# Transposing q, k and x in whole 128x128 blocks instead of 64x64 quarters, in a fused attention and mixture kernel

## The chip, the cores and the metric

The kernel runs on one core of a Trainium2 chip. The metric is the device time of one execution in microseconds (us), lower is better. A core has five engines that work side by side, each through a queue of its own in order: TensorE (PE, matrix products), ScalarE (ACT), VectorE (DVE), GpSimd (POOL) and SyncE (SP, which here only issues transfers). Matrix products read SBUF and write PSUM, a small memory of eight banks; ACT and DVE carry results from PSUM back to SBUF.

## The reference, cut to what matters

Three stages follow one another: an attention with decay over 4 batches, 8 heads, 768 tokens and 64 channels, a soft mixture of 8 experts, and a feed-forward layer with a gate. The change touches the first.

```python
for b in range(nb):                       # 12 blocks of 64 tokens
    intra = einsum('bhic,bhjc->bhij', qb, kb) * Dmask
    intra = einsum('bhij,bhjd->bhid', intra, vb)
    inter = einsum('bhid,bhde->bhie', qb * lam_pow, kv_state)
    out[:, :, sl] = intra + inter
    kv_state = lam_block * kv_state + einsum('bhsd,bhse->bhde', kb * rev_pow, vb)
x = out.transpose(0, 2, 1, 3).reshape(B * S, H * D)      # 3072 x 512
logits = x @ phi                                          # 32 slots, 4 for each of 8 experts
slot_input = softmax(logits, 0).T @ x                     # experts: relu(. @ w1[e]) @ w2[e]
x = softmax(logits, 1) @ slot_out
h = x @ w_in
out = (h * sigmoid(1.702 * h)) @ w_out
```

The scores need q and k with the channels on the partitions, though they lie in memory with the tokens there, so both are transposed on TensorE. The attention's result comes out with channels on the partitions and is transposed back.

## The kernel before

The attention is a loop of 48 steps. A step is 256 tokens of one batch and two heads: two chunks (c) of 128 tokens, each as two subs of 64 partitions by even and odd token. The loop is a pipeline written out by hand: iteration i works on steps i-1, i, i+1 and i+2 at once, and the order of the calls in it is the order of each engine's queue. On TensorE an iteration is, in this order:

- do_SC(i+1), L262: scores of step i+1 from qkT, the transposed q and k. do_ST(i+1), L278: what the step adds to the state, from kd (k times the decay) and v. Both write the banks bs.
- do_T(i+2), L235: q and k of step i+2 are transposed by products with an identity, 16 of them, each on one 64x64 quarter of the array, into the banks bt.
- do_XS(i), L301: q times the state, into the banks bx.
- do_XT(i-1), L327: the result x of step i-1 is transposed back, 8 products on quarters, into other columns of the same bt.
- in six of every eight iterations a piece of the mixture's head: L345 (logits), L355, L379, L394, L423 and L408.
- do_XA(i), L316: scores times v, into bx.

Around it ACT copies bt to qkT (take_T, L240) and to xn (take_XT, L335) and bx to xT (L321); DVE masks the scores (AT, L269) and adds the states (L285 to L291); POOL makes qdT (do_qd, L247) and kd (do_kd, L253), and a part of an early conversion of late weights in every fourth iteration (L195, L196). SP issues all loads: q, k and v of later steps, pieces of the expert weights w (NPC of them within the loop), and stage for the conversion. make_dec (L478, L481) fills the decay masks in the first iterations.

TensorE's float32 products are each two pairs of a weight load and a matmul in the trace (768 records at L316 for 8 products in 48 steps), a transpose through PE.transpose is one pair (20 records at L355 for 4 in 5 calls).

After the loop come the experts (L723, L745) and the feed-forward layer (L919, L966). The change leaves them as they are, but for one weight piece that is loaded a little later.

Of the kernel before, what the change touches and what calls it, by code (L numbers as in the profile page):

```python
# [8 lines left out]
F32 = mybir.dt.float32  # L9
F32R = mybir.dt.float32r  # L10
U32 = mybir.dt.uint32
AF = mybir.ActivationFunctionType
# [5 lines left out]
def attention_moe_gelu_kernel(  # L18
# [14 lines left out]
    PE, ACT, DVE, POOL, SP = nc.tensor, nc.scalar, nc.vector, nc.gpsimd, nc.sync  # L33

    B, H, S, D = q.shape
    P = 128
    NHP = H // 2
    HS = 384
    BT = 256
# [13 lines left out]
    NG = NBLK // UB  # L53
    NSTEP = NBLK * NHP
    NE = 1
    NPC = 31
    NPC_B = 6
    NPC_C = 4
    EPS = 1e-9
    TG = 2 * HS  # L60
# [22 lines left out]
    early = early_cm.__enter__()  # L83

    def bank(tag, name):
        return psp.tile([P, 512], F32, tag=tag, name=name)

    def banks(tag, name):
        return psp.tile([P, 2, 512], F32, tag=tag, name=name)

    ident = const.tile([P, P], F32, name="ident")
# [3 lines left out]

    dec = early.tile([P, H, 2, P], F32, name="dec", bufs=1)
    qtab = early.tile([P, NHP, 2, D], F32, name="qtab", bufs=1)
    for tag, n, bufs in (("kd", BT, 2), ("qkT", 2 * BT, 2), ("k", BT, 4), ("q", BT, 4)):
        early.tile([P, n], F32, tag=tag, name="room", bufs=bufs)
    c_nat = const.tile([P, NT // P, NS], F32, name="c_nat")  # L100
    acc = const.tile([P, DM], F32, name="acc")
# [8 lines left out]
    q_t, k_t, v_t = {}, {}, {}  # L110
# [6 lines left out]
    def load_step(s, what="qkv"):  # L117
        if s >= NSTEP:
            return
        b, bb, hp, blk = step_of(s)  # L120
        for src, nm, ts, bufs, pool in ((q, "q", q_t, 4, early), (k, "k", k_t, 4, early), (v, "v", v_t, 5, attn)):
            if nm in what:
                t = ts[s] = pool.tile([P, 2, 2 * D], F32, tag=nm, name=nm, bufs=bufs)
                SP.dma_start(out=t, in_=src[b, 2 * hp:2 * hp + 2, bb * BT:(bb + 1) * BT, :]
                             .rearrange("h (p s) d -> p h (s d)", s=2))
# [99 lines left out]


    s_mid, s_end = {}, {}
    qkT, qdT, kd, AT, xT, xn = {}, {}, {}, {}, {}, {}

    def do_T(s, bt):  # L230
        for j, src in enumerate((q_t[s], k_t[s])):
            for sub in range(2):
                for c in range(2):
                    for h in range(2):
                        PE.matmul(bt[HR[h], c, (2 * j + sub) * D:(2 * j + sub + 1) * D],  # L235
                                  src[HR[c], h, sub * D:(sub + 1) * D], ident[HR[c], HR[c]], start=True, stop=True)

    def take_T(s, bt):
        t = qkT[s] = early.tile([P, 2, 2, 2, D], F32, tag="qkT", name="qkT", bufs=2)
        ACT.activation(out=t.rearrange("m c j s p -> m c (j s p)"), in_=bt[:, :, :4 * D], func=AF.Copy)  # L240

    def do_qd(s):
        if s < 0 or s >= NSTEP:
# [6 lines left out]
    def do_kd(s):  # L250
        b, bb, hp, blk = step_of(s)
        kd[s] = early.tile([P, 2, 2, D], F32, tag="kd", name="kd", bufs=2)
        POOL.tensor_tensor(out=kd[s], in0=k_t[s].rearrange("q h (s d) -> q h s d", s=2),  # L253
                           in1=dec[:, 2 * hp:2 * hp + 2, :, P - 1:P].to_broadcast([P, 2, 2, D]), op=ALU.mult)

    HR = [slice(h * D, (h + 1) * D) for h in range(2)]
# [24 lines left out]
    def do_state(s, bs):  # L281
        b, bb, hp, blk = step_of(s)
        s_mid[s] = attn.tile([P, D], F32, tag="sm", name="sm")
        if bb == 0:
            DVE.tensor_copy(out=s_mid[s], in_=bs[:, 0, 2 * P:2 * P + D])  # L285
        else:
            DVE.scalar_tensor_tensor(out=s_mid[s], in0=s_end[s - NHP], scalar=qtab[:, hp, 1, D - 1:D],
                                     in1=bs[:, 0, 2 * P:2 * P + D], op0=ALU.mult, op1=ALU.add)
        if bb < NB - 1:
            s_end[s] = attn.tile([P, D], F32, tag=f"se{hp}", name="se")  # L290
            DVE.scalar_tensor_tensor(out=s_end[s], in0=s_mid[s], scalar=qtab[:, hp, 1, D - 1:D],  # L291
                                     in1=bs[:, 1, 2 * P:2 * P + D], op0=ALU.mult, op1=ALU.add)
# [27 lines left out]
        xT[s] = tailp.tile([P, 2, P], F32, tag="xT", name="xT", bufs=NHP + 1)  # L320
        ACT.activation(out=xT[s], in_=bx[:, :, :P], func=AF.Copy)  # L321

    def do_XT(s, bt):
        for c in range(2):
            for u in range(2):
                for h in range(2):
                    PE.matmul(bt[HR[u], h, (4 + c) * D:(5 + c) * D], xT[s][HR[h], c, HR[u]], ident[HR[h], HR[h]],  # L327
                              start=True, stop=True)

    def take_XT(s, bt):  # L330
        b, bb, hp, blk = step_of(s)
        g, half = divmod(blk, UB)
        if hp == 0 and half == 0:
            xn[g] = tailp.tile([P, R, NHP, P], F32, tag="xn", name="xn")
        ACT.activation(out=xn[g][:, 2 * half:2 * half + 2, hp].rearrange("p c (h d) -> p h c d", h=2),  # L335
                       in_=bt[:, :, 4 * D:6 * D].rearrange("p h (c d) -> p h c d", c=2), func=AF.Copy)


    RS = R * NS
# [111 lines left out]
    with tc.manual_schedule():  # L451
# [36 lines left out]
        n = 1  # L488
# [3 lines left out]
            n *= 2  # L492
        load_step(1, "v")
        load_step(2, "qk")
        POOL.memset(ones, 1.0)

        def make_isum():
# [10 lines left out]
        for i in range(-2, NSTEP):  # L508
            g, ph = divmod(i, PH)
            if i == 1:  # L510
                make_isum()
            if 0 < i + 2 < NHP:
                for h in range(2):
                    make_dec(2 * (i + 2) + h)

            load_step(i + 5, "qk")
            load_step(i + 4, "v")
            load_pieces(i)
            if i == -2:
                SP.dma_start(out=phi_sb, in_=phi.rearrange("(k p) s -> p k s", p=P))  # L520
            c, turn = divmod(i - 2, EVERY)
            if turn == 1 and 0 <= c + 1 < len(EARLY):
                load_early(c + 1)

            bs, bt, bx = banks("s", "bs"), banks("t", "bt"), banks("x", "bx")
            if 0 <= i + 1 < NSTEP:
                do_SC(i + 1, bs)
                do_ST(i + 1, bs)
                take_SC(i + 1, bs)
                do_state(i + 1, bs)  # L530
            if 0 <= i + 2 < NSTEP:
                do_T(i + 2, bt)
                if i == -2:
                    warm_up(1)
            if 0 <= i < NSTEP:
                fence = do_XS(i, bx)
            if 0 <= i - 1 < NSTEP:
                do_XT(i - 1, bt)
            if 0 <= i + 2 < NSTEP:
                take_T(i + 2, bt)  # L540
            if 0 <= i - 1 < NSTEP:
                take_XT(i - 1, bt)
            do_qd(i + 1)
            if 0 <= i + 2 < NSTEP:
                do_kd(i + 2)
            if ph == 0 and 0 <= g - 1 < NG:
                tail_logits(g - 1, 1)
            if ph == 4 and 0 <= g < NG:
                tail_logits(g, 0)
            if ph == 1 and 0 <= g - 1 < NG:  # L550
                tail_L(g - 1)
            if ph == 2 and 0 <= g - 1 < NG:
                tail_max(g - 1)
            if ph == 3 and 0 <= g - 1 < NG:
                tail_exp(g - 1)
            if ph == 5 and 0 <= g - 1 < NG:
                tail_z(g - 1)
                tail_slot(g - 1)
            if i == NSTEP - 1:
                tail_logits(NG - 1, 1, NHP - 1)  # L560

            if 0 <= i < NSTEP:
                do_XA(i, bx, fence)
            if ph == 5 and 0 <= g - 1 < NG:
                tail_acc(g - 1)

            if turn == 0 and 0 <= c < len(EARLY):
                do_early(c)
            if ph == 4 and 0 <= g - 1 < NG:
                tail_row(g - 1)  # L570
            if ph == 6 and 0 <= g - 1 < NG:
                tail_row_exp(g - 1)
            if i == NSTEP - 2:
                early_cm.__exit__(None, None, None)
                slotb_cm = tc.tile_pool(name="slotb", bufs=NPC_B, side="right", reuse_waits="tile")
                slotb = slotb_cm.__enter__()

                rooms = [piece_room(NPC + j) for j in reversed(range(NPC_B))]
                while rooms:
                    load_piece(rooms.pop())  # L580
            if i == NSTEP - 1:
                attn_cm.__exit__(None, None, None)
                slotc_cm = tc.tile_pool(name="slotc", bufs=NPC_C, side="left", reuse_waits="tile")
                slotc = slotc_cm.__enter__()
                for _ in range(NPC_C):
                    load_piece()
# [48 lines left out]
        DVE.tensor_reduce(out=cm, in_=bL[:, :RS].rearrange("p (c s) -> p s c", c=R), axis=AX.X, op=ALU.max)  # L635
        L = tl["L", g] = tailp.tile([P, R, NS], F32, tag="lp", name="L", bufs=1)
        DVE.tensor_copy(out=L, in_=bL[:, :RS].rearrange("p (c s) -> p c s", c=R))
        bt = banks("t", "bt")
        do_XT(NSTEP - 1, bt)
        take_XT(NSTEP - 1, bt)  # L640
        psa_cm.__exit__(None, None, None)
        psp = ctx.enter_context(tc.tile_pool(name="psp", bufs=1, space=bass.MemoryType.PSUM, reuse_waits="tile"))

# [443 lines left out]
```

## Time and profile before

| what | us |
|---|---|
| median of three runs (543.84 to 546.93) | 545.87 |
| the profiled execution's own time | 546.3 |
| its span, first to last instruction | 544.5 |
| TensorE busy (92% of the span) | 498.2 |
| VectorE, ScalarE, GpSimd busy | 251.7, 240.6, 91.8 |
| mean granted TensorE clock, as a share of full | 0.971 |

A busy TensorE is one on which some matmul is shown to run; the ends of matmuls are modelled, and a stall begins within such an end. "Issue" in a row is time in which an engine waited for nothing that the profile shows.

### The profile page before, as it was taken

What the parts mean: (1) busy time and instruction counts of PE and PEld (TensorE: products, weight loads), DVE (VectorE), ACT (ScalarE), POOL (GpSimd) and SP (SyncE); (2) the same over time, 40 slices, a digit from 0 to 9 for tenths busy, and PEclk for the clock granted to TensorE, in tenths of its full rate; (3) what the DMA queues carried; (4) which work ended last, traced back from release to release, by engine and by line L of the source; (5) the groups of instructions that cost most, each with busy time, mean ns of one, the idle gap of its engine ahead of it and who ended that gap; (6) DMA issues with size and microseconds to landing.
All of it is one profiled execution on the core that took longest, in us unless ns stands there. A gap on an engine that the chain in (4) does not pass through costs nothing.

```text
span 544.5 us, 15920 instructions
## 1 busy us (share of the span) xinstructions
PE 498.2 (92%) x6846; PEld 392.3 (72%) x6846; DVE 251.7 (46%) x503; ACT 240.6 (44%) x495; POOL 91.8 (17%) x166
## 2 busy tenths in 40 slices
PE   5778787988877789999999999999999999999997
PEld 3667676776756564447878778888888888888886
DVE  5543344454535332128979999732225222522222
ACT  3433333434323332348768777543333333333333
POOL 3544544545435311000000000000000000000000
PEclk7899999989989988999999999999999999999999
DMA  6587766778757598983444353030003000300003
GB/s 172 147 250 203 232 203 200 211 224 250 203 173 201 175 334 321 395 333 108 125 154 153 119 155 116 0 117 0 1 0 117 1 2 0 117 0 1 0 1 116
DMA packets 62150, 76.60 MB, mean 141 GB/s; under 512 B 4992, under 2 KB 42112, under 8 KB 62080
## 3 DMA queue, kind: packets, MB, share of 16 engines
q1 hardware_dynamic: 61936, 75.58, 43.6%
q8 instruction: 54, 0.88, 0.7%
q14 instruction: 16, 0.13, 0.1%
q10 hardware_dynamic: 144, 0.00, 0.0%
HBM read 69.28 MB, written 6.29 MB: 139 GB/s over the span
## 4 chain that ended last, share of the span: by engine, by line
PE 78%; issue 10%; POOL 5%; DVE 4%; ACT 1%; DMA 1%; POOLq 0%; ACTq 0%; DVEq 0%
PE bo L966 47%; PE bhh L919 4%; PE bh L723 3%; PE bx L316 3%; PE bt L235 3%; PE bs L262 3%; PE bacc L745 3%; PE bx L301 2%; PE bs L278 2%; PE bt L327 2%; POOL qdT L247 2%; POOL kd L253 1%; PE bl L345 1%; DVE seeds L478 1%; POOL isum L500 1%
## 5 line engine op out<-in xcount | busy, mean ns | idle before, releaser
L966 PE MATMUL bo<-whi,ghi 128*128 128x512 f32 x382 | 150.1, 395 | 0.1
L966 PE MATMUL bo<-whi,glo 128*128 128x512 f32 x382 | 149.7, 394 | 0.0
L966 PE MATMUL bo<-wlo,ghi 128*128 128x512 f32 x382 | 148.9, 391 | 0.1
L933 DVE TENSOR_TENSOR glo<-g,ghi 128x768 fp32r<-128x768 f32 x64 | 61.2, 956 | 132.4 <-ACT ghi L930 132.3
L927 ACT ACTIVATE g<-bhh 128x384 f32<-128x384 f32 x128 | 56.2, 489 | 125.9 <-PE bhh L919 125.8
L966 PEld LDWEIGHTS bo<-whi,glo 128*128 128x128 f32 x382 | 71.7, 188 | 16.7 <-DVE glo L933 0.3
L966 PEld LDWEIGHTS bo<-wlo,ghi 128*128 128x128 f32 x382 | 71.7, 188 | 16.3 <-issue 2.5
L966 PEld LDWEIGHTS bo<-whi,ghi 128*128 128x128 f32 x382 | 71.7, 188 | 13.9 <-DVE W2s L877 0.5
L240 ACT ACTIVATE qkT<-bt 128x512 f32<-128x512 f32 x48 | 28.8, 599 | 100.9 <-PE bt L327 99.3
L269 DVE TENSOR_TENSOR AT<-bs,dec 128x512 f32<-128x512 f32 x48 | 32.9, 686 | 67.2 <-PE bs L278 67.2
L930 ACT ACTIVATE ghi<-g 128x768 fp32r<-128x768 f32 (+1 forms) x65 | 54.4, 836 | 2.1
L247 POOL TENSOR_TENSOR qdT<-qkT,qtab 128x256 f32<-128x256 f32 x48 | 35.0, 730 | 51.2 <-ACT qkT L240 47.3
L262 PE MATMUL bs<-qkT 64*64 64x128 f32 x768 | 33.0, 286 | 10.5 <-ACT qkT L240 8.9
L327 PE MATMUL bt<-ident,xT 64*64 64x64 f32 x768 | 31.9, 234 | 7.7 <-issue 7.7
L316 PE MATMUL bx<-AT,v 64*64 64x128 f32 x768 | 35.5, 291 | 1.0 <-issue 0.6
L262 PEld LDWEIGHTS bs<-qkT 64*64 64x64 f32 x768 | 23.1, 138 | 16.0 <-ACT qkT L240 12.9
L919 PE MATMUL bhh<-cT,W2s 128*128 128x384 f32 x128 | 33.3, 338 | 0.0
L316 PEld LDWEIGHTS bx<-AT,v 64*64 64x64 f32 x768 | 23.4, 139 | 13.5 <-issue 11.9
L235 PE MATMUL bt<-ident,k 64*64 64x64 f32 x768 | 24.3, 229 | 8.5 <-issue 8.5
L253 POOL TENSOR_TENSOR kd<-k,dec 128x256 f32<-128x256 f32 x48 | 29.8, 621 | 9.1 <-ACT dec L481 6.5
L278 PE MATMUL bs<-v,kd 64*64 64x64 f32 x640 | 23.2, 231 | 8.2 <-issue 4.7
L327 PEld LDWEIGHTS bt<-ident,xT 64*64 64x64 f32 x768 | 24.8, 136 | 7.3 <-issue 7.3
(167 smaller groups left out, 633.3 us busy)
## 6 DMA issues: line engine op xcount, KB each, us to landing
w<-in_moe_w_dram SPq DMA_DIRECT2D x64, 512.0 KB, 5.2
f<-in_moe_w_out_dram SPq DMA_DIRECT2D x15, 512.0 KB, 3.6
q<-in_q_dram SPq DMA_DIRECT2D x48, 128.0 KB, 4.0
k<-in_k_dram SPq DMA_DIRECT2D x48, 128.0 KB, 3.7
v<-in_v_dram SPq DMA_DIRECT2D x48, 128.0 KB, 3.4
f<-in_moe_w_in_dram SPq DMA_DIRECT2D x12, 512.0 KB, 3.8
out_dram<-o SPq DMA_DIRECT2D x23, 256.0 KB, 2.1
stage<-in_moe_w_in_dram SPq DMA_DIRECT2D x8, 256.0 KB, 4.3
```

Source lines behind the costliest of these rows:

```text
L235: PE.matmul(bt[HR[h], c, (2 * j + sub) * D:(2 * j + sub + 1) * D], src[HR[c], h, sub * D:(sub + 1) * D], ident[HR[c], HR[c]], start=True, ...
L247: POOL.tensor_tensor(out=qdT[s], in0=qkT[s][:, :, 0], in1=qtab[:, hp, None].to_broadcast([P, 2, 2, D]), op=ALU.mult)
L253: POOL.tensor_tensor(out=kd[s], in0=k_t[s].rearrange("q h (s d) -> q h s d", s=2), in1=dec[:, 2 * hp:2 * hp + 2, :, P - 1:P].to_broadcast( ...
L262: PE.matmul(bs[HR[c], h, sj * P:(sj + 1) * P], qkT[s][HR[h], c, 1, sj], qkT[s][HR[h], c, 0].rearrange("m s p -> m (s p)"), start=True, sto ...
L278: PE.matmul(bs[HR[h], c, 2 * P:2 * P + D], kd[s][HR[c], h, sj, :], v_t[s][HR[c], h, sj * D:(sj + 1) * D], start=(sj == 0), stop=(sj == 1), ...
L316: mm = PE.matmul(bx[HR[h], c, :P], v_t[s][HR[c], h, sj * D:(sj + 1) * D], AT[s][HR[c], h, sj, :], start=(sj == 0 and c + bb == 0), stop=(s ...
L327: PE.matmul(bt[HR[u], h, (4 + c) * D:(5 + c) * D], xT[s][HR[h], c, HR[u]], ident[HR[h], HR[h]], start=True, stop=True)
L919: PE.matmul(bh[j][u][:, :HS], W2s[:, f * P:(f + 1) * P], cT[tg // (NTG // 2)][:, t0:t0 + HS], start=True, stop=True)
L927: ACT.activation(out=g[j][:, u * HS:(u + 1) * HS], in_=bh[j][u][:, :HS], func=AF.Gelu_apprx_sigmoid)
L930: ACT.activation(out=ghi[j][:, o], in_=g[j][:, o], func=AF.Copy)
L933: DVE.tensor_tensor(out=glo[j][:, o], in0=g[j][:, o], in1=ghi[j][:, o].bitcast(F32), op=ALU.subtract)
L966: PE.matmul(ob[t], a[j][:, t * P:(t + 1) * P], w[f], start=(begin and i == 0), stop=(end and i == 2))
```

## The change

q and k of a step are copied (do_qk), q by ACT and k by DVE, into a tile qk in which the 64 channels of both heads of a token stand side by side. A transpose of 128 tokens by 128 of these columns then gives both heads at once, so do_T is four whole 128x128 transposes and do_XT two. Each has a bank of its own (t and xt), where both shared the two banks bt. On TensorE do_T moves behind do_XS; on ACT take_T stands right behind do_T, take_XT moves behind the copy of xT, and the copy of q follows it; POOL's do_kd reads qk. q and k are loaded one step earlier, and one weight piece moves from the loop to its end.

```diff
-    NPC = 31
-    NPC_B = 6
+    NPC = 30
+    NPC_B = 7
...
-    def do_T(s, bt):
-        for j, src in enumerate((q_t[s], k_t[s])):
+    def do_qk(s):
+        if s >= NSTEP:
+            return
+        t = qk[s] = early.tile([P, 2, 2, 2, D], F32, tag="qk", name="qk", bufs=2)
+        ACT.activation(out=t[:, 0].rearrange("q s h d -> q h s d"),
+                       in_=q_t[s].rearrange("q h (s d) -> q h s d", s=2), func=AF.Copy)
+        DVE.tensor_copy(out=t[:, 1].rearrange("q s h d -> q h s d"),
+                        in_=k_t[s].rearrange("q h (s d) -> q h s d", s=2))
+
+    def do_T(s):
+        bt = bank("t", "bt")
+        for j in range(2):
             for sub in range(2):
-                for c in range(2):
-                    for h in range(2):
-                        PE.matmul(bt[HR[h], c, (2 * j + sub) * D:(2 * j + sub + 1) * D],
-                                  src[HR[c], h, sub * D:(sub + 1) * D], ident[HR[c], HR[c]], start=True, stop=True)
-
-    def take_T(s, bt):
+                PE.transpose(bt[:, (2 * j + sub) * P:(2 * j + sub + 1) * P],
+                             qk[s][:, j, sub].rearrange("q h d -> q (h d)"), ident)
         t = qkT[s] = early.tile([P, 2, 2, 2, D], F32, tag="qkT", name="qkT", bufs=2)
-        ACT.activation(out=t.rearrange("m c j s p -> m c (j s p)"), in_=bt[:, :, :4 * D], func=AF.Copy)
+        ACT.activation(out=t.rearrange("m c j s p -> m c (j s) p"),
+                       in_=bt.rearrange("m (j c p) -> m c j p", j=4, c=2), func=AF.Copy)
...
-        POOL.tensor_tensor(out=kd[s], in0=k_t[s].rearrange("q h (s d) -> q h s d", s=2),
+        POOL.tensor_tensor(out=kd[s], in0=qk[s][:, 1].rearrange("q s h d -> q h s d"),
...
-    def do_XT(s, bt):
+    def do_XT(s):
+        bt = bank("xt", "bxt")
         for c in range(2):
-            for u in range(2):
-                for h in range(2):
-                    PE.matmul(bt[HR[u], h, (4 + c) * D:(5 + c) * D], xT[s][HR[h], c, HR[u]], ident[HR[h], HR[h]],
-                              start=True, stop=True)
+            PE.transpose(bt[:, c * P:(c + 1) * P], xT[s][:, c], ident)
+        return bt
...
-            load_step(i + 5, "qk")
+            load_step(i + 6, "qk")
...
-            if 0 <= i + 2 < NSTEP:
-                do_T(i + 2, bt)
-                if i == -2:
-                    warm_up(1)
             if 0 <= i < NSTEP:
                 fence = do_XS(i, bx)
+            if 0 <= i + 2 < NSTEP:
+                do_T(i + 2)
+                if i == -2:
+                    warm_up(1)
             if 0 <= i - 1 < NSTEP:
-                do_XT(i - 1, bt)
-            if 0 <= i + 2 < NSTEP:
-                take_T(i + 2, bt)
-            if 0 <= i - 1 < NSTEP:
-                take_XT(i - 1, bt)
+                bt = do_XT(i - 1)
...
             if 0 <= i < NSTEP:
                 do_XA(i, bx, fence)
+            if 0 <= i - 1 < NSTEP:
+                take_XT(i - 1, bt)
+            do_qk(i + 3)
```

On TensorE's queue one iteration in the middle of the loop, before:

```order
L262 MATMUL bs<-qkT 64x128 x8
L278 MATMUL bs<-v,kd 64x64 x4
L235 MATMUL bt<-ident,q 64x64 x8
L235 MATMUL bt<-ident,k 64x64 x8
L301 MATMUL bx<-qdT,se 64x128
L301 MATMUL bx<-qdT,sm 64x128
L327 MATMUL bt<-ident,xT 64x64 x8
L316 MATMUL bx<-AT,v 64x128 x8
```

And the same iteration of the changed kernel:

```order
L269 MATMUL bs<-qkT 64x128 x8
L285 MATMUL bs<-v,kd 64x64 x4
L308 MATMUL bx<-qdT,se 64x128
L308 MATMUL bx<-qdT,sm 64x128
L243 MATMUL bt<-ident,qk 128x128 x4
L333 MATMUL bxt<-ident,xT 128x128 x2
L361 MATMUL bL<-ident,lp 128x128 x4
```

The pair of L301 (now L308) stands twice in each iteration and is shown once. The 16 products of L235 became four of L243, behind do_XS; the 8 of L327 became two of L333. L361 is the head's piece of this iteration (L355 before), and do_XA (L323) follows it as before.

On ACT one iteration with a logits copy (lp), with the engines whose semaphores each row waits for, before:

```order
L240 ACTIVATE qkT<-bt 128x512 [waits PE_49,Activation_49,Pool_49]
L335 ACTIVATE xn<-bt 128x2x2x64
L350 ACTIVATE lp<-bl 128x256 [waits PE_49]
L321 ACTIVATE xT<-bx 128x256 [waits PE_49]
L240 ACTIVATE qkT<-bt 128x512 [waits PE_49,Pool_49]
```

And after:

```order
L246 ACTIVATE qkT<-bt 128x512 [waits PE_49,Activation_49,Pool_49]
L356 ACTIVATE lp<-bl 128x256 [waits PE_49]
L328 ACTIVATE xT<-bx 128x256 [waits PE_49]
L341 ACTIVATE xn<-bxt 128x2x128
L234 ACTIVATE qk<-q 128x2x2x64 [waits DVE_49,DMAHW5_49,Activation_49,Pool_49]
L246 ACTIVATE qkT<-bt 128x512 [waits PE_49,Pool_49]
```

The copy of xn moved behind that of xT, and the new copy of q (L234) stands between it and the next iteration's qkT.

## Rows read from the trace of the kernel before

**Rows 1.** Busy time by engine, granted clock, DMA share: the loop, then the experts.

```profile
20.00:197.00 177.00, 141.81 (x4714) 117.79 (x4703) 79.80 (x207) 63.42 (x173) 79.58 (x124) 0.96 0.72 210
197.00:243.00 46.00, 45.07 (x492) 20.91 (x492) 10.01 (x41) 15.26 (x33) 3.69 (x12) 0.89 0.97 368
```

**Rows 2.** TensorE's waits from 20 to 197 us: total, times, longest.

```profile
PE bt L235 <- issue: 10.4, 9, 1.7
PE bt L327 <- issue: 7.7, 5, 1.8
PE bs L278 <- issue: 4.7, 5, 1.3
PE bs L278 <- POOL kd L253: 3.5, 5, 1.8
PE bs L262 <- ACT qkT L240: 3.1, 10, 0.4
PE bl L345 <- issue: 2.0, 1, 2.0
```

**Rows 3.** TensorE's timeline around three stalls: start, us, what, idle before.

```profile
35.00 0.27 PE L278 MATMUL bs<-v,kd 64*64 64x64 f32 x3
36.57 0.39 PE L278 MATMUL bs<-v,kd 64*64 64x64 f32 x11 [1.30 <-issue]
...
41.38 0.40 PE L235 MATMUL bt<-ident,k 64*64 64x64 f32 x12 [1.30 <-issue]
...
46.77 0.35 PE L327 MATMUL bt<-ident,xT 64*64 64x64 f32 x9 [1.61 <-issue]
```

**Rows 4.** Work from the end of one stall to the next (columns of Rows 1).

```profile
36.57:41.38 4.81, 3.20 (x126) 2.82 (x127) 3.10 (x8) 1.47 (x4) 1.48 (x2) 1.00 0.78 208
41.38:46.77 5.39, 3.47 (x126) 3.09 (x127) 0.88 (x2) 1.15 (x3) 2.66 (x5) 1.00 0.81 252
```

**Rows 5.** The page: instructions of each engine, and the instruction queue (packets, MB).

```profile
PE 498.2 (92%) x6846; PEld 392.3 (72%) x6846; DVE 251.7 (46%) x503; ACT 240.6 (44%) x495; POOL 91.8 (17%) x166
...
q8 instruction: 54, 0.88, 0.7%
```

**Rows 6.** The chain that ended last, in iterations without a stall: start, us, what.

```profile
48.95 0.47 PE bt L235 x30
49.42 0.32 PE bx L301 x6
...
49.80 0.28 PE bt L327 x11
50.07 0.59 PE bL L355 x4
50.66 0.60 PE bx L316 x16
51.26 0.44 PE bs L262 x16
51.69 0.17 PE bs L278 x6
...
53.30 0.60 PE bx L316 x16
```

**Rows 7.** ACT's timeline: two operations of 128x256, one behind the other.

```profile
25.36 0.38 ACT L321 ACTIVATE xT<-bx 128x256 f32<-128x256 f32 x1
25.64 0.44 ACT L173 ACTIVATE w_in<-stage 128x256 f32<-128x256 f32 x1
```

**Rows 8.** ACT's slowest copy of 128x256, by line: busy, mean ns, idle before.

```profile
L481 ACT ACTIVATE dec<-seeds 128x256 f32<-128x256 f32 x8 | 5.2, 656 | 9.8 <-DVE seeds L478 9.8
```

**Rows 9.** A stretch at the lower clock (columns of Rows 1).

```profile
21.75:25.16 3.41, 3.13 (x84) 2.87 (x84) 2.16 (x6) 0.58 (x2) 1.49 (x3) 0.50 0.43 116
```

**Rows 10.** TensorE's timeline in that stretch.

```profile
22.03 0.70 PE L278 MATMUL bs<-v,kd 64*64 64x64 f32 x16 [1.80 <-POOL kd L253]
...
24.22 1.07 PE L316 MATMUL bx<-AT,v 64*64 64x128 f32 x14
```

More of the change, by code (lines that the diff above doesn't have):

```diff
@@ L97, in attention_moe_gelu_kernel @@
     qtab = early.tile([P, NHP, 2, D], F32, name="qtab", bufs=1)
-    for tag, n, bufs in (("kd", BT, 2), ("qkT", 2 * BT, 2), ("k", BT, 4), ("q", BT, 4)):
+    for tag, n, bufs in (("kd", BT, 2), ("qkT", 2 * BT, 2), ("qk", 2 * BT, 2), ("k", BT, 4), ("q", BT, 4)):
         early.tile([P, n], F32, tag=tag, name="room", bufs=bufs)
@@ L227, in attention_moe_gelu_kernel @@
     s_mid, s_end = {}, {}
-    qkT, qdT, kd, AT, xT, xn = {}, {}, {}, {}, {}, {}
-    def do_T(s, bt):
-        for j, src in enumerate((q_t[s], k_t[s])):
-            for sub in range(2):
-                for c in range(2):
-                    for h in range(2):
-                        PE.matmul(bt[HR[h], c, (2 * j + sub) * D:(2 * j + sub + 1) * D],
-                                  src[HR[c], h, sub * D:(sub + 1) * D], ident[HR[c], HR[c]], start=True, stop=True)
-    def take_T(s, bt):
+    qk, qkT, qdT, kd, AT, xT, xn = {}, {}, {}, {}, {}, {}, {}
+    def do_qk(s):
[9 more added lines that the diff above has]
+        for j in range(2):
+            for sub in range(2):
+                PE.transpose(bt[:, (2 * j + sub) * P:(2 * j + sub + 1) * P],
+                             qk[s][:, j, sub].rearrange("q h d -> q (h d)"), ident)
         t = qkT[s] = early.tile([P, 2, 2, 2, D], F32, tag="qkT", name="qkT", bufs=2)
-        ACT.activation(out=t.rearrange("m c j s p -> m c (j s p)"), in_=bt[:, :, :4 * D], func=AF.Copy)
+        ACT.activation(out=t.rearrange("m c j s p -> m c (j s) p"),
+                       in_=bt.rearrange("m (j c p) -> m c j p", j=4, c=2), func=AF.Copy)
     def do_qd(s):
@@ L334, in take_XT @@
             xn[g] = tailp.tile([P, R, NHP, P], F32, tag="xn", name="xn")
-        ACT.activation(out=xn[g][:, 2 * half:2 * half + 2, hp].rearrange("p c (h d) -> p h c d", h=2),
-                       in_=bt[:, :, 4 * D:6 * D].rearrange("p h (c d) -> p h c d", c=2), func=AF.Copy)
+        ACT.activation(out=xn[g][:, 2 * half:2 * half + 2, hp], in_=bt[:, :BT].rearrange("p (c d) -> p c d", c=2),
+                       func=AF.Copy)
     RS = R * NS
@@ L494, in attention_moe_gelu_kernel @@
         load_step(2, "qk")
+        load_step(3, "qk")
+        do_qk(0)
         POOL.memset(ones, 1.0)
@@ L523, in attention_moe_gelu_kernel @@
                 load_early(c + 1)
-            bs, bt, bx = banks("s", "bs"), banks("t", "bt"), banks("x", "bx")
+            bs, bx = banks("s", "bs"), banks("x", "bx")
             if 0 <= i + 1 < NSTEP:
@@ L530, in attention_moe_gelu_kernel @@
                 do_state(i + 1, bs)
+            if 0 <= i < NSTEP:
+                fence = do_XS(i, bx)
             if 0 <= i + 2 < NSTEP:
-                do_T(i + 2, bt)
+                do_T(i + 2)
                 if i == -2:
                     warm_up(1)
-            if 0 <= i < NSTEP:
-                fence = do_XS(i, bx)
             if 0 <= i - 1 < NSTEP:
-                do_XT(i - 1, bt)
-            if 0 <= i + 2 < NSTEP:
-                take_T(i + 2, bt)
-            if 0 <= i - 1 < NSTEP:
-                take_XT(i - 1, bt)
+                bt = do_XT(i - 1)
             do_qd(i + 1)
@@ L637, in attention_moe_gelu_kernel @@
         DVE.tensor_copy(out=L, in_=bL[:, :RS].rearrange("p (c s) -> p c s", c=R))
-        bt = banks("t", "bt")
-        do_XT(NSTEP - 1, bt)
-        take_XT(NSTEP - 1, bt)
+        take_XT(NSTEP - 1, do_XT(NSTEP - 1))
         psa_cm.__exit__(None, None, None)
```

## The prediction

> **What bounds the kernel now.** I read the busy table by stage first. The loop runs from the start to about 197 us, and the change lies in it. From 20 to 197 us TensorE is busy 141.8 of 177.0 us, VectorE 79.8, ScalarE 63.4, GpSimd 79.6, and the DMA engines 0.72 [rows 1]. No engine is full, TensorE is the nearest, and it idles 35.2 us.
>
> The list of waits tells what TensorE idles for: four rows "issue" make 24.8 us in 20 events, against 3.5 us for kd from POOL and 3.1 us for qkT from ACT [rows 2]. So the largest idle time waits for no other engine. The timeline shows what kind it is: stalls of 1.30, 1.30 and 1.61 us, in the middle of a run of equal products, at L278, then L235, then L327 [rows 3]. A data wait would sit at the first product of a group; these sit anywhere. What they have in common is their distance: from the end of one stall to the end of the next stand 126 matmuls and 127 weight loads, both times, in 4.81 and 5.39 us [rows 4]. The page has 54 packets on the instruction queue, 0.88 MB in all, so 16 KB each, and 13,692 matmul and load records of TensorE, 254 for each packet [rows 5]. I read this as TensorE waiting for its own instructions: a packet holds about 253 records, and where they run out sooner than about 4.8 to 5.4 us, TensorE stands.
>
> How fast the loop would go without that, the chain shows in a stretch without stalls: do_XA starts at 50.66 and again at 53.30, 2.64 us an iteration with a small piece of the head in it [rows 6]. The mean is 177.0/46 = 3.85 us.
>
> **The change, term by term**, over the 46 steps of the stretch.
>
> Instructions. An iteration has (4714 + 4703)/46 = 205 records of TensorE [rows 1]. do_T goes from 16 products of two pairs (64 records) to four single pairs (8), do_XT from 32 to 4: 84 fewer, 121 left. A packet of 253 then lasts 2.1 iterations where it lasted 1.2. At 2.64 us or more an iteration that is at least 5.5 us, over the 4.81 and 5.39 us that a packet took when TensorE stood for it. So I let the stalls go: 24.8 us, and 0.2 us more for each of the 20, since the three products before a stall show 0.27 us, nearly all a modelled end in which others would have started [rows 3]. **-29**. The bounds: all of it, or a share as in the first rival.
>
> [...]
>
> Clock. The loop's mean clock is 0.96 [rows 1]; at the lower level of 0.50 that is 14 us of the stretch, which cost up to half, 7 us. One such stretch follows a wait of 1.80 us on POOL, which stays [rows 9, 10]. I take the others to follow stalls: **-4** (0 to -7).
>
> qkT. take_T waited for both do_T and do_XT, since they shared bt. Now it may start at do_T's end, with do_XT and do_XA (0.60 [rows 6]) still to run while it takes its time. **-3**, the wait of row L262 [rows 2].
>
> The transposes. On the chain do_T and do_XT are 0.47 + 0.28 = 0.75 us. The four 128x128 transposes of L355 took 0.59 us from first start to do_XA's start, with a change of tile shape before and behind them [rows 6]. Six cost at most 0.59 x 6/4 = 0.89; if 0.15 of the 0.59 is for the changes, 0.66 + 0.15 = 0.81. I take +0.06 an iteration, **+3** (0 to +6).
>
> The copy of q. It stands in ACT's queue behind xT and xn, and do_T, first of the moved group, waits for it. ACT starts xT 0.07 us after do_XA's modelled end (25.36 after 24.22 + 1.07 [rows 7, 10]). Operations of this size start 0.28 us apart, and one from SBUF takes 0.44 us [rows 7], so q is ready 0.07 + 0.28 + 0.28 + 0.44 = 1.07 us after. TensorE, which starts its next product within that end, some 0.1 to 0.2 us before it is over, needs 0.44 for the scores, 0.17 for the state (twice that with 8 products), 0.32 for do_XS [rows 6], with the change of shape some 0.95 us from the end on. The wait is 0.1 us, **+5**. Its bounds: nothing, where the head's pieces delay TensorE, or 0.35 us if this copy costs 0.656 like the slowest of its size [rows 8], +16. Behind the waiting transpose stand do_XT and do_XA, so the whole iteration shifts. ACT and DVE have room for one copy more a step [rows 1]; DVE's copy of k is due a transpose later, behind two reductions in one iteration of eight.
>
> GpSimd. kd needs the copy of k, made an iteration earlier, so nothing new is waited for. But POOL's share of the early conversion already makes TensorE wait 3.5 us in 5 events [rows 2], and a faster loop meets it sooner: **+3** (0 to +8).
>
> Start and end. The first do_T waits for two copies more, and one 512 KB weight piece moves behind the loop, where the DMA engines are busy 0.97 [rows 1]: **+2** (0 to +4). The loop's loads are the same bytes in less time: 0.72 x 177/154 = 0.83, under the 0.97 that the experts' stage reaches, so no term. q and k are now released by their copies and loaded a step earlier.
>
> Sum: -29 - 4 - 3 + 3 + 5 + 3 + 2 = -23 us. The profiled execution's 546.3 becomes 523; it lies 0.4 us over the median, so the median is forecast at 523 too. With every addition at nothing and the clock's whole 7 us it is 546.3 - 39 = 507. The forecast's own range is 513 to 533.
>
> **Rivals.**
>
> *The copies cost nothing (507 to 513).* Speaks for it: six of eight iterations have a piece of the head, during which ACT catches up. Against: do_T's wait comes before that piece. Around 509.
>
> *Packets still run out.* If a packet's delay begins only when the one before is nearly used up, each crossing stalls as now, and only the crossings get fewer: 121/205 = 59% remain. The terms are -12, 0 for the clock, -3, +3, +2 (the wait for q hides behind stalls), +3, +2: -5, so 541. For it: the stalls appear with 4.81 and with 5.39 us alike [rows 4]. Against: with 20 events in a stretch that used some 37 packets' worth of records (9,417/253), nearly half the crossings show none.
>
> *The changes of shape empty the array.* Were each of the two an iteration to cost a small product's modelled 0.27 us [rows 3], that is 2 x 0.27 x 46 = 25 us in place of +3: 545, no change. Against it stands L355, which goes through the same two changes with four transposes in 0.59 us [rows 6]. [...]
>
> [...]
>
> *The issue waits are something else* than instructions, and stay: 523 + 29 + 4 = 556. Against: the same distance in records twice, which is a packet's.
>
> **Chances.** The forecast 0.65; copies for nothing 0.12; packets still run out 0.11; emptied array 0.03; clock 0.06; something else 0.03. 0.5% is 2.7 us, about what a measurement of this kernel tells from no change. 541 with some spread lies on both sides of it, so I split it in 0.06 faster and 0.05 same. Faster: 0.65 + 0.12 + 0.06 = 0.83. Same: 0.05 + 0.03 = 0.08. Slower: 0.06 + 0.03 = 0.09. The range goes from 508, near the sum without additions, to 541, the case where packets still run out; about half of that case, the last three, and a little below are left out, some 0.2.
>
> **What the changed profile would show.** Right: about 4,000 fewer records on each count together and some 38 packets on the instruction queue; "issue" rows of TensorE in the loop down from 24.8 us to under 6; the loop's end near 174 us instead of 197; a new row in which the transposes (L243) wait for ACT's copy of q, a few us in all; do_SC's wait for qkT gone; do_T, do_XT and the changes of shape around 0.8 us. Wrong: issue waits of over 1 us at half the crossings; a clock under 0.9 over the loop; do_T waiting 0.3 us or more in each iteration; or the experts starting early and then waiting for weights, which would give the gain back behind the loop.

## The result, and the profile after

The changed kernel took 524.09 us (median of four runs, 521.85 to 524.74); the kernel before, on the same chip, 546.4 (543.84 to 547.62). The ratio is 0.959, with a 95% interval of 0.954 to 0.964, so 22 us less. The forecast was 523. Medians here and below are of all runs, while ratios and intervals leave out one slow run each of two later kernels: 558.3 us where the fastest took 548.17, and 532.9 where it took 524.48. The profiled execution took 524.62 us with a span of 522.8, at a mean granted clock of 0.987.

The page of the changed kernel, instructions of each engine and the instruction queue, as [rows 5]:

```profile
PE 494.4 (95%) x4830; PEld 378.0 (72%) x4830; DVE 262.9 (50%) x551; ACT 258.5 (49%) x543; POOL 92.0 (18%) x166
...
q8 instruction: 38, 0.62, 0.5%
```

2,016 matmuls and as many weight loads are gone, and 16 packets. The loop now ends earlier: the last do_XA starts at 174.88 us instead of 195.75, the first at 14.80 instead of 14.72. So the loop gives 20.9 of the 21.7 us that the span lost, and nothing is lost behind it. Its busy times, in the columns of [rows 1]:

```profile
20.00:175.00 155.00, 137.62 (x2827) 104.84 (x2829) 90.98 (x253) 80.13 (x217) 80.23 (x127) 0.98 0.79 235
```

TensorE idles 17.4 us here, where it idled 35.2 of 177.0; it is busy 4.2 us less. What it idles for, all of its rows from 20 to 175 us, as [rows 2]:

```profile
PE bs L285 <- POOL kd L260: 10.9, 11, 1.6
PE bs L269 <- DVE se L298: 2.4, 2, 1.2
PE bs L269 <- ACT xn L341: 1.5, 2, 0.8
PE bs L269 <- ACT qkT L246: 0.6, 2, 0.4
PE bx L308 <- ACT xT L328: 0.6, 1, 0.6
```

No "issue" row is left. Before, there were the four of [rows 2] with 24.8 us and three smaller ones, 26.9 us in 24 events together:

```profile
PE bx L301 <- issue: 0.9, 1, 0.9
PE bx L316 <- issue: 0.6, 2, 0.3
PE bs L262 <- issue: 0.6, 1, 0.6
```

What these 24 stalls wait for stands in the trace of the kernel before, in the times of the packets on the instruction queue. All 24 stand at the same place of a packet: counted in all records of TensorE's queue, its few semaphore records among them, they are whole multiples of 256 apart, give or take one. And each ends 1.2 to 1.6 us after a packet has landed. The steps from one packet to the next (crossings) that show no stall mostly hang on the packet too: of the 37 crossings between 20 and 197 us, 31 come within 1.7 us of the landing. The prediction took these for free. From crossing to crossing it is 4.7 us in the mean (3.6 to 6.2). In the changed kernel it is 6.7 us, and at each of 22 crossings the packet had landed at least 2.8 us before.

The wait for qkT fell from 3.1 to 0.6 us. The wait for kd from POOL grew from 3.5 to 10.9. It sits in every fourth iteration, behind POOL's share of the early conversion. The chain that ended last shows such a place (start, us, what):

```profile
40.35 0.86 POOL w_in L195
...
41.28 0.73 POOL w_in L196
...
42.01 0.68 POOL qdT L254
...
42.70 0.59 POOL kd L260
...
43.33 0.27 PE bs L285 x2
```

Four operations of POOL stand in a row, and do_ST comes last. Right behind it the same chain shows an iteration in which TensorE sets the pace:

```profile
45.58 0.60 PE bx L323 x16
46.18 0.44 PE bs L269 x16
46.62 0.22 PE bs L285 x8
46.84 0.50 PE bx L308 x8
47.34 0.59 PE bt L243 x4
47.92 0.22 PE bxt L333 x2
48.14 0.45 PE bL L361 x4
```

do_T and do_XT take 0.59 + 0.22 = 0.81 us here. The head's piece behind them (L361) is on whole blocks too, so the change of shape back comes behind that. Where do_XA follows directly, its first start is 0.80 us behind do_T's. From one do_XA to the next it is 2.55 to 3.0 us, 3.6 in one iteration of eight, and 4.4 to 6.7 in the iterations with the conversion.

### The profile page after: what moved, and what is told of

Its sections match the earlier page's. It is cut to its first block, busy times and chain, and to the rows that moved or that the text cites. A ratio compares the mean times of both kernels' runs of the same rounds, so it can differ in the third digit from the quotient of the medians.

```text
span 522.8 us, 12000 instructions
## 1 busy us (share of the span) xinstructions
PE 494.4 (95%) x4830; PEld 378.0 (72%) x4830; DVE 262.9 (50%) x551; ACT 258.5 (49%) x543; POOL 92.0 (18%) x166
## 4 chain that ended last, share of the span: by engine, by line
PE 79%; POOL 7%; DVE 5%; issue 5%; ACT 3%; DMA 1%; SPq 0%; POOLq 0%; ACTq 0%; DVEq 0%
PE bo L971 49%; PE bhh L924 4%; PE bt L243 4%; PE bh L728 3%; PE bacc L750 3%; PE bx L323 3%; PE bx L308 2%; POOL qdT L254 2%; POOL kd L260 2%; PE bs L285 1%; PE bl L351 1%; PE bs L269 1%; PE bxt L333 1%; POOL w_in L195 1%; POOL w_in L196 1%
## 5 line engine op out<-in xcount | busy, mean ns | idle before, releaser
L254 POOL TENSOR_TENSOR qdT<-qkT,qtab 128x256 f32<-128x256 f32 x48 | 35.2, 734 | 28.4 <-ACT qkT L246 28.3
L243 PE MATMUL bt<-ident,qk 128*128 128x128 f32 x192 | 34.4, 300 | 4.7 <-ACT qk L234 3.1
L269 PE MATMUL bs<-qkT 64*64 64x128 f32 x768 | 31.3, 278 | 6.0 <-DVE se L298 2.4
L323 PE MATMUL bx<-AT,v 64*64 64x128 f32 x768 | 33.2, 284 | 0.8 <-ACTq L311 0.8
L260 POOL TENSOR_TENSOR kd<-qk,dec 128x256 f32<-128x256 f32 x48 | 30.1, 627 | 16.6 <-DVE qk L236 12.5
L243 PEld LDWEIGHTS bt<-ident,qk 128*128 128x128 f32 x192 | 21.1, 146 | 16.0 <-ACT qk L234 7.4
L323 PEld LDWEIGHTS bx<-AT,v 64*64 64x64 f32 x768 | 21.1, 134 | 15.5 <-issue 13.9
L285 PE MATMUL bs<-v,kd 64*64 64x64 f32 x640 | 20.8, 227 | 10.9 <-POOL kd L260 10.9
L924 PEld LDWEIGHTS bhh<-cT,W2s 128*128 128x128 f32 x128 | 23.9, 188 | 5.4
```

What stands on the lines that cost most here:

```text
L243: PE.transpose(bt[:, (2 * j + sub) * P:(2 * j + sub + 1) * P], qk[s][:, j, sub].rearrange("q h d -> q (h d)"), ident)
L254: POOL.tensor_tensor(out=qdT[s], in0=qkT[s][:, :, 0], in1=qtab[:, hp, None].to_broadcast([P, 2, 2, D]), op=ALU.mult)
L260: POOL.tensor_tensor(out=kd[s], in0=qk[s][:, 1].rearrange("q s h d -> q h s d"), in1=dec[:, 2 * hp:2 * hp + 2, :, P - 1:P].to_broadcast([P ...
L269: PE.matmul(bs[HR[c], h, sj * P:(sj + 1) * P], qkT[s][HR[h], c, 1, sj], qkT[s][HR[h], c, 0].rearrange("m s p -> m (s p)"), start=True, sto ...
L323: mm = PE.matmul(bx[HR[h], c, :P], v_t[s][HR[c], h, sj * D:(sj + 1) * D], AT[s][HR[c], h, sj, :], start=(sj == 0 and c + bb == 0), stop=(s ...
L924: PE.matmul(bh[j][u][:, :HS], W2s[:, f * P:(f + 1) * P], cT[tg // (NTG // 2)][:, t0:t0 + HS], start=True, stop=True)
```

## The experiments

Each was timed beside the kernel before. Times below are medians, with the ratio and its interval against the kernel before.

**x alone.** Only do_XT is changed; q and k stay on quarters, nothing is copied, the banks bt stay shared. An iteration then has 205 - 28 = 177 records.

```diff
-            for u in range(2):
-                for h in range(2):
-                    PE.matmul(bt[HR[u], h, (4 + c) * D:(5 + c) * D], xT[s][HR[h], c, HR[u]], ident[HR[h], HR[h]], ...)
+            PE.transpose(bt[:, 0, (4 + 2 * c) * D:(6 + 2 * c) * D], xT[s][:, c], ident)
```

> The kernel before with one part of the change: only x is transposed whole, two transposes in place of 8 products, in the same place of the order and in the same banks; q and k stay on quarters and no copy is added. TensorE's records fall from 205 to 177 an iteration, so a packet of 253 lasts 1.43 iterations instead of 1.23. Instructions run out (my theory): a packet takes at least 4.8 to 5.4 us when TensorE stands for it, so an iteration needs 3.4 to 3.8 us where it took 3.85; 8 to 18 us faster than before, issue waits of TensorE in the loop down from 24.8 us to 8 to 17. Rival, the gain of the whole change came from the new order, the separate banks and the earlier copy of qkT: at most 0.1 us an iteration from the shorter transposes, 0 to 4 us faster, issue waits unchanged near 25 us.

528.18 us, 0.966 (0.960 to 0.972): a third of the records removed, and 18 of the 22 us. TensorE's largest waits from 20 to 197 us in this kernel:

```profile
PE bs L278 <- POOL kd L253: 5.6, 9, 1.8
PE bt L235 <- issue: 5.4, 8, 1.1
...
PE bx L316 <- issue: 0.9, 3, 0.4
```

With three more of 0.7, 0.5 and 0.2, issue makes 7.7 us in 14 events, of 26.9 in 24, just under what was expected. So the stalls get fewer and shorter. The gain is not in proportion to the records: most of it comes with the first of them. The loop still hangs on its packets: in its 32 crossings up to 177 us the packet had landed within 1.7 us in 23, and they are 4.8 us apart.

**q and k alone.** q and k are copied and transposed whole, x stays on quarters, the banks stay shared (ACT copies qkT in two operations): 149 records.

> The other part of the change alone: q and k copied and transposed whole as in the changed kernel and in its order, x on 64x64 quarters as before, both in the two shared banks bt (so ACT takes qkT in two operations of 256 columns). 149 records an iteration, a packet of 253 lasts 1.7 iterations, 4.9 us at the changed kernel's 2.9 without the conversion: just at the 4.8 to 5.4 us. Instructions run out: nearly all stalls go, as with x alone, 523 to 531 us, issue waits in the loop under 6 us; the two parts, 18 us for x alone, do not add. Rival, each part brings its own gain and they add: 524.1 + 17.8, so 540 to 546 us.

531.67 us, 0.973 (0.967 to 0.979), just over what was expected. Issue is down to 0.6 us, the wait for kd is 7.9 in 11 events. At 149 records the packets no longer set the pace: one crossing of 27 came within 1.7 us of the landing. So q and k alone take nearly all of the stalls away and x alone most of them, and their gains, 14 and 18 us, don't add up: both together give 22.

**Records put back.** Into the changed kernel go 42 products of one column in each iteration, 84 records, so that it has as many as before, with little work in them; in a second kernel 8 products of 192 columns, 16 records, with more work. The columns they write are read by nobody.

```diff
                 do_ST(i + 1, bs)
+                for n in range(42):
+                    pc, ph_ = divmod(n % 4, 2)
+                    PE.matmul(bs[HR[ph_], pc, 448:449], warm[HR[pc], :D], warm[HR[pc], :1], start=True, stop=True)
```
```diff
                 do_ST(i + 1, bs)
+                for n in range(8):
+                    PE.matmul(bs[HR[0], 0, 320:512], warm[HR[0], :D], warm[HR[0], :192], start=True, stop=True)
```

> The changed kernel with 42 products of one column in bf16 on 64x64 quarters behind the state's products of each iteration, written to columns of the bank that nobody reads: 84 records more, so 205 an iteration as before the change, and some 0.5 us of TensorE time. Instructions run out: a packet lasts 1.2 iterations again, so an iteration takes 3.9 to 4.4 us against 3.4 in the changed kernel; 550 to 575 us, and issue waits of TensorE in the loop of 15 us or more, spread over any line. Rival, the number of records does not matter: only the 0.5 us of TensorE time, less where the iteration waits for GpSimd anyway, 540 to 548 us, no issue waits over 0.5 us.

> The control for the one with 42 small products: 8 products of 192 columns in bf16 on one quarter in the same place, some 0.6 us of TensorE time, but only 16 records more. Instructions run out: 137 records an iteration, a packet lasts 1.85 iterations, 6 us or more, so no issue waits and the products' own time alone, 540 to 552 us, clearly faster than the one with 42 small products. Rival, records do not matter: this one is as slow as the other or slower, its products being the longer ones.

With 42 short products: 551.36 us, 1.008 (1.004 to 1.012). With 8 long ones: 542.3, 0.992 (0.988 to 0.995). The page of the first counts `PE 515.6 (94%) x6846` and again 54 packets; the second has 520.9 us busy, x5214 and 41 packets. The one in which TensorE is less busy is 9 us slower. Its waits from 20 to 200 us have the stalls again, half of their time in the added products, which wait for no data:

```profile
PE bs L539 <- issue: 9.0, 10, 2.2
PE bs L285 <- POOL kd L260: 4.4, 7, 1.1
PE bs L285 <- issue: 4.1, 4, 1.4
PE bs L269 <- issue: 1.6, 1, 1.6
```

With three smaller ones that is 17.3 us of issue in 18 events. All 18 stand again at the end of a packet of 256 and end 1.2 to 1.6 us after a packet's landing, so it isn't that short products are slow to start. The second kernel has no issue row; its largest wait is kd with 6.3. This is the experiment that decides for the number of records: the same transposes, copies and banks, and the stalls are back.

**The conversion off POOL.** Its comparison and product (L195, L196) become one operation of DVE.

```diff
-        by_turns(conversion(("early", c), o, POOL))
+        by_turns(conversion(("early", c), o, DVE))
```

> The changed kernel with the last part of the early conversion (two operations on GpSimd, 0.85 and 0.73 us) as one operation on VectorE instead. In the changed kernel every fourth iteration, the one with that conversion, takes 4.4 us or more where its neighbours take 2.6 to 3.6, with TensorE waiting for kd 10.9 us in all. Theory, with instructions no longer short GpSimd's queue in those iterations is what bounds the loop: 8 to 18 us faster than the changed kernel, 506 to 516 us, and the waits for kd under 3 us. Rival, the iterations are long for the conversion's own transfer or VectorE's part of it: 0 to 4 us.

521.77 us, 0.953 (0.948 to 0.959): a miss. The wait for kd fell to 1.9 us, but another took its place, TensorE's from 20 to 175 us:

```profile
PE bs L269 <- DVE se L298: 6.9, 6, 2.1
PE bs L269 <- DVE sm L294: 2.4, 2, 1.8
PE bs L285 <- POOL kd L260: 1.9, 2, 1.6
```

do_SC now waits for the state's operations, which stand behind the conversion on DVE. All the rest of the conversion was in that iteration too, and the ten iterations with it still take 3.3 to 5.5 us, 4.5 in the mean where it was 4.9.

**The conversion spread over two iterations.** ACT's part, two of DVE's three operations and POOL's comparison stay where they were; DVE's third and POOL's product move to the next iteration, and the next part is loaded an iteration later. It is put into the changed kernel, into the kernel before and into the one with x alone. The main lines:

```diff
-        by_turns(conversion(("early", c), o, POOL))
+        work = early_work[c] = conversion(("early", c), o, None)
+        m = o
+        next(work)
+        next(work)
+        POOL.tensor_scalar(out=m, in0=m, scalar1=F64_MIN, scalar2=None, op0=ALU.is_ge)
...
+    def end_early(c):
+        o = EARLY[c][-1]
+        next(early_work[c], 0)
+        next(early_work[c], 0)
+        POOL.tensor_tensor(out=o, in0=stage[:, 2 * CB:3 * CB].bitcast(F32), in1=o, op=ALU.mult)
...
-            if turn == 1 and 0 <= c + 1 < len(EARLY):
+            if turn == 2 and 0 <= c + 1 < len(EARLY):
```

> The changed kernel with the early conversion spread over two iterations: in the first the absolute value, two of VectorE's three operations and GpSimd's first, in the next the third and GpSimd's second, and the next part's load an iteration later. Neither queue gets more than 1.2 us of it in one iteration. Theory, the long iterations (4.4 to 6.7 us, every fourth) come from the conversion standing in one piece ahead of the loop's own work in the queues of VectorE and GpSimd: they fall to 3.3 us or less and the time to 506 to 515 us. Rival, they are long for something else that comes every fourth iteration, such as the 256 KB load of the stage or a busy DMA: 520 to 525 us.

> The kernel before with the same spread conversion. If instructions bound its loop, a wait taken away turns into a longer stall at the next packet: 0 to 5 us faster than before, 541 to 546 us, and issue waits above 24.8 us. Rival, waits and stalls add up: as much faster as the changed kernel is by the same edit, 9 to 18 us.

> x alone whole (177 records an iteration) with the spread conversion. A packet lasts 1.43 iterations, so an iteration cannot go much under 3.4 us on the mean; it has 3.46 now. Instructions run out: 0 to 6 us faster than x alone without the spreading, 522 to 528 us, and more issue waits; clearly slower than the whole change with the same spreading. Rival, records no longer bind at 177: 510 to 518 us, as the whole change.

The changed kernel: 515.58 us, 0.943 (0.939 to 0.948), 8.5 under it without the spreading. The iterations with the conversion come down from 4.4 to 6.7 us to 3.6 to 4.8, less far than expected; the wait for kd goes from 10.9 to 5.0. The kernel before: 544.56, 0.997 (0.994 to 1.000), no change that can be told. x alone: 528.19, 0.962 (0.955 to 0.970), the same as without. In these two POOL's wait does fall, from 3.5 and 5.6 to 2.0 us in each. TensorE's waits from 20 to 197 us in the kernel before with spreading:

```profile
PE bt L247 <- issue: 12.3, 8, 2.0
PE bs L290 <- issue: 6.8, 7, 1.8
PE bt L339 <- issue: 3.8, 4, 2.1
...
PE bl L357 <- issue: 2.0, 1, 2.0
PE bs L290 <- POOL kd L265: 2.0, 2, 1.8
```

Four issue rows with 24.9 us, and three smaller: 27.1 us, where it was 26.9. Here there was only 1.5 us of POOL's wait to gain, and where that went the rows don't show. With x alone they do: issue grew from 7.7 to 12.1 us while kd fell from 5.6 to 2.0. The 3.6 us of wait taken away came back as 4.4 us of stalls, as is to be expected if the packets set the pace. At 121 records they no longer set it, and the same edit is worth 8.5 us. So 177 records are still bound by packets, though little shows in their "issue" rows as long as something else is late too; the crossings show it, 23 of 32 within 1.7 us of the landing with the spreading as without.

**do_T at its old place.** In the changed kernel do_T moves ahead of do_XS again. That makes the wait for the copy of q longer, and adds two changes of tile shape to each iteration.

```diff
+            if 0 <= i + 2 < NSTEP:
+                do_T(i + 2)
             if 0 <= i < NSTEP:
                 fence = do_XS(i, bx)
-            if 0 <= i + 2 < NSTEP:
-                do_T(i + 2)
```

> The changed kernel with the transposes of q and k in their old place on TensorE, ahead of do_XS instead of behind it. My term for the copy of q: it is ready some 1.07 us after do_XA's end, and a transpose that stands 0.3 to 0.5 us earlier waits as much longer, in iterations that do not wait for GpSimd or for the clock: 8 to 18 us slower than the changed kernel, 532 to 542 us, and the weight loads of these transposes wait 20 us or more for ACT's copy of q where they waited 7.4. Rival, the place does not matter since ACT's order lets the copy through in time: 523 to 526 us.

540.45 us, 0.989 (0.983 to 0.995), as expected, and 16 us of the 22 are gone. The transposes' weight loads wait 16.6 us for the copy of q, where 20 or more were expected. TensorE's waits from 20 to 175 us, its timeline in one iteration (columns of [rows 3]), and the chain that ended last in the same place:

```profile
PE bt L243 <- ACT qk L234: 12.5, 30, 0.4
```
```profile
46.74 0.40 PE L285 MATMUL bs<-v,kd 64*64 64x64 f32 x8
47.56 0.66 PE L243 MATMUL bt<-ident,qk 128*128 128x128 f32 x4 [0.42 <-ACT qk L234]
```
```profile
46.83 0.38 ACT xn L341
47.21 0.31 ACT qk L234
...
47.56 0.66 PE bt L243 x4
48.22 0.58 PE bx L308 x8
```

The copies of xn and q on ACT are on the path now, and TensorE's work begins again when q is ready. The wait is 12.5 us; that for kd is 7.4 instead of 10.9. So of the 16 us about 7 are left, which hold the added changes of shape and were not measured apart.

**The copy of q in two other ways,** on top of the changed kernel with spreading: on ACT ahead of xn, or on DVE like that of k.

```diff
-        ACT.activation(out=t[:, 0].rearrange("q s h d -> q h s d"),
-                       in_=q_t[s].rearrange("q h (s d) -> q h s d", s=2), func=AF.Copy)
+        DVE.tensor_copy(out=t[:, 0].rearrange("q s h d -> q h s d"),
+                        in_=q_t[s].rearrange("q h (s d) -> q h s d", s=2))
```

> The changed kernel with the spread conversion (515.6 us), and on ACT the copy of q ahead of that of xn. The copy of q is ready 0.28 us sooner, and the wait of the transposes' weight loads for it (7.5 us in 33 events, 0.23 each) goes: 4 to 9 us faster, 507 to 512 us. Rival, that wait lies within the drain of do_XS's products, which the transposes of another tile shape must await anyway: 0 to 2 us, 513 to 516 us.

> The changed kernel with the spread conversion, and both copies on VectorE: q no longer stands behind ACT's copies of x. VectorE's copy of 128x256 takes 0.29 us (median), up to 0.84 where GpSimd works at the same time. If the wait for q counts: 4 to 9 us faster than 515.6 less what VectorE's longer queue costs in iterations with reductions, 507 to 514 us. Rival, VectorE is late with the state and the masks instead: 515 to 520 us, and do_SC's wait for VectorE over 5 us.

Ahead of xn: 514.87 us, 0.942 (0.937 to 0.947), 0.7 under 515.58 and within what the runs scatter. On DVE: 513.12, 0.939 (0.933 to 0.945), 2.5 under, the fastest kernel of this study and 11 us under the changed one; kd's wait there is 2.5 us, and the transposes wait 1.8 for the copy on DVE. The 2.5 us are just at what can be told: no run of one is within the runs of the other, but they were timed on two chips, and the intervals overlap.

## Why the prediction was right

The time came out 1 us from the forecast, by the mechanism it named. That it is so close is in part luck: four of its terms were off and made up for each other.

**Instructions (-29).** Right. The four rows of 24.8 us [rows 2] are gone, and three smaller ones. That it was the number of records is shown by putting them back, which brought 17.3 us of issue and a time over that of the kernel before, by the place of every stall at the end of a packet, and by the spreading, which gains 8.5 us in the changed kernel and nothing that can be told where packets bind. What the prediction did not see is that the gain comes with the first records removed: with 177 or 149 left most stalls are gone, at 177 in part because other waits stand in their place. It also had 4.8 to 5.4 us for a packet from two stalls; over the loop it is 4.7, and the crossings that it counted against its rival as free mostly were not. The rival "packets still run out" is ruled out for 121 records, where no such row is left and no crossing comes close to the packet's landing. At 205 there were stalls of up to 2.0 us before, and of up to 2.2 us with the records put back.

**Clock (-4).** Right in kind. The loop's mean went from 0.96 [rows 1] to 0.98. From 20 us on four stretches of 3.4 us at 0.50 became two; the last three of the four came behind stalls of 1.65, 1.59 and 1.80 us. At the level of 0.50 that is 14 and 7 us, and half of the difference, 3 to 4 us, is an estimate of the most that it can cost. It was not measured apart. A lower clock over the loop, given 0.06, did not come.

**qkT (-3).** Right: 3.1 us became 0.6.

**The transposes (+3).** Right: 0.8 us on the chain, as forecast, against 0.75 [rows 6]. That is not all that the changes of shape cost: in the changed kernel do_T never starts less than 0.20 us after the last product of do_XS does, while from one of its transposes to the next it is 0.11 us (median, from 20 to 175 us). In ten iterations TensorE shows no gap in either kernel, and there the changed one is 0.14 us longer in the mean: 0.03 to 0.33 us longer in eight, 0.05 and 0.06 shorter in two. Over the 36 iterations without the conversion that makes 5 us, an estimate, for the transposes and the copy of q together, where the forecast had 8. The rival of an emptied array, 0.5 us more in each iteration, is ruled out by the same numbers.

**The copy of q (+5).** Mis-sized: about 1 us. The weight loads do wait for it; TensorE's products have no such row, from 20 to 175 us, only eight gaps of 0.14 us ahead of do_T that are too short for one:

```profile
PEld bt L243 <- ACT qk L234: 7.4, 32, 0.4
```

This wait lies mostly in the time in which, by their modelled ends, do_XS's products are still running. The step that failed is the estimate that TensorE would be ready 0.1 us before q. TensorE's and ACT's timeline show do_XA, the copy of q and do_T in one iteration of the changed kernel:

```profile
45.51 0.67 PE L323 MATMUL bx<-AT,v 64*64 64x128 f32 x16
...
47.27 0.66 PE L243 MATMUL bt<-ident,qk 128*128 128x128 f32 x4
```
```profile
46.79 0.42 ACT L234 ACTIVATE qk<-q 128x256 f32<-128x256 f32 x1
```

The half on ACT was right: q is ready 1.03 us after do_XA's modelled end, where 1.07 was forecast. TensorE was put at 0.95. But do_T starts at 1.09 where nothing else is late, and so it does in most iterations with the copy ahead of xn, where q is ready at 0.75. Only where do_XS has 4 records instead of 8, in a third of the iterations, does it then start earlier, at 0.87. That fits the 0.7 us that moving the copy gained. The mechanism itself is there, as do_T at its old place shows with 12.5 us.

**GpSimd (+3).** Mis-sized: the wait for kd grew by 7.4 us, just inside the bound of 8. The prediction let a faster loop meet the conversion "sooner", and did not reckon how much of it had been hidden by stalls: the iterations with it took 3.2 to 5.4 us before and take 4.4 to 6.7 now. With it came 3 us more of waits that the sum did not have, mostly for se and xn. Spreading the conversion took 8.5 us off the time. POOL is so the next limit in one iteration of four, but not alone, as the move to DVE showed.

**Start and end (+2).** Nothing: the first do_XA is 0.1 us later, and behind the loop the kernel is no slower.

What can be added up from rows are TensorE's waits from 20 us to the loop's end. Issue gives -26.9 us, qkT -2.5, kd +7.4, the other rows +2.8 (from 1.7 to 4.5), and gaps too short for a row +1.4, together -17.8. TensorE is busy 4.2 us less; in this lie the clock, the transposes and the modelled ends that hid part of each stall, and the rows don't tell them apart. That makes the 22 us.

Not settled: why the spread conversion still leaves those iterations at 3.6 to 4.8 us, what a change of shape costs by itself (the 0.15 us in the prediction was its author's estimate), and what sets the 4.7 us of a packet.

## What to carry to other kernels

Where stalls without a releaser fall in the middle of equal products, count the records between them. Here the same number each time spoke for instruction supply; fewer and larger instructions then gained 22 us, while taking away another wait gained nothing that can be told (0.997, 0.994 to 1.000). The times of the packets on the instruction queue settled it: each stall ended 1.2 to 1.6 us after a landing. The stalls also hid the next limit, the wait for kd, which was 3.5 us before and 10.9 after, so look up which waits lie just under the stalls and size them anew for the faster loop. Two ways of removing the stalls did not add up, 14 and 18 us making 22; the cheaper gave most of it, x alone with 18 us, a few lines and no copy. But its loop stayed bound by packets, and the spreading that then gained 8.5 us in the changed kernel gained nothing in it.

## What the runs showed of the hardware

A packet of 16 KB, 256 records of TensorE's queue, cost time in these runs only where it was used up fast. With 205 matmul and load records in an iteration stalls of up to 2.2 us appeared, each ending 1.2 to 1.6 us after a packet's landing, and the packets were used up at 4.7 us each; with 177 it was 4.8, and when another wait was taken away stalls took its place; with 121 it was 6.7, and there was no stall.

In the changed kernel DVE's copy of k took 0.40 to 0.84 us where it began inside a product of two tensors on POOL, and 0.29 and 0.32 where it began inside a comparison. Two of its places, POOL's and DVE's timeline (start, us, what):

```profile
40.35 0.85 POOL L195 TENSOR_SCALAR w_in<-w_in 128x256 f32<-128x256 f32 x1 [2.84 <-ACT w_in L173]
...
68.79 0.73 POOL L254 TENSOR_TENSOR qdT<-qkT,qtab 128x256 f32<-128x256 f32 x1
```
```profile
40.58 0.32 DVE L236 COPY qk<-k 128x256 f32<-128x256 f32 x1
...
68.90 0.77 DVE L236 COPY qk<-k 128x256 f32<-128x256 f32 x1
```

The copy that began inside POOL's comparison took 0.32 us, near the usual 0.29. The one inside its product took 0.77 and ended 0.15 us after that product did. Of the nine copies that began inside a product of two tensors on POOL, eight ended 0.15 us after it and the ninth after the next one; of the two that began inside a comparison, both ended before it. But with the spreading one copy that began inside a comparison took 0.51 us and ended 0.15 us after it. Why these copies took longer was not shown; no experiment here took this apart.
